# First chunks' queries in two loads, w_out's first piece ungated, and a moved conversion of w_in

## The chip, the cores and the metric

One core of a Trainium2 chip runs the kernel. The metric is the device time of one execution in microseconds (us), lower is better; the time of a kernel is the median of several runs. A core has five engines with an instruction queue each, which it works off in order: TensorE (PE, matmuls; PEld in the profile is its weight loads), VectorE (DVE), ScalarE (ACT), GpSimd (POOL) and SyncE (SP, which here issues nearly all transfers). They meet through semaphores. Tiles lie in SBUF (128 partitions), matmul results in PSUM banks.

## The reference: what is computed

The inputs are float32, except the two weight matrices: the reference multiplies them by a float64 scalar, so they arrive in 64 bits and the kernel converts them itself. An attention with sketched polynomial features is followed by an MLP with exact gelu:

```python
batch, n_heads, seq, head_dim = (4, 4, 1088, 32)     # r = 8 rows in S1 and S2
def phi(x):
    a = np.einsum('rd,bhsd->bhsr', S1, x)
    b = np.einsum('rd,bhsd->bhsr', S2, x)
    return np.einsum('bhsi,bhsj->bhsij', a, b).reshape(*x.shape[:-1], r * r)
q_p, k_p = (phi(q), phi(k))
kv = np.einsum('bhsf,bhsd->bhfd', k_p, v)
z = np.sum(k_p, axis=2)
num = np.einsum('bhsf,bhfd->bhsd', q_p, kv)
den = np.einsum('bhsf,bhf->bhs', q_p, z)[..., None] + 1e-06
x = (num / den).transpose(0, 2, 1, 3).reshape(B * S, H * D)      # 4352 x 128
h = x @ w_in                                                     # w_in 128 x 2048
g = 0.5 * h * (1.0 + erf(h / sqrt(2)))
out = g @ w_out                                                  # w_out 2048 x 128
```

The sum over the sequence needs every key and value of a batch element; each token of the queries is then independent.

## The kernel before

**Tiling.** The 1024 first tokens of each of the four batch elements are worked on in chunks of 512, two for each element (eight "main" chunks, numbered 0 to 7; 0 and 1 belong to element 0); the last 64 tokens of all elements make a ninth chunk. For each chunk the attention result `xT` (128 features x 512 tokens) is multiplied with w_in in 16 blocks of 128 hidden features (`hidden`, L715), ACT takes each block through gelu (L728), and the blocks are multiplied with w_out (`project`, L847, for the first blocks of chunks 0 and 1; products of a fast scheme, `two_products`, L794, for the others). `hidden` has two PSUM banks (`hidden_bank`, L77): the matmul of a block waits until the gelu of the block two before it has read its bank.

**Order.** The text of the kernel is the order on each engine: at the end (L1217 to L1224) each instruction is made to follow the one before it on its engine. The prologue (L887 to L961) is written out by hand, then a list of steps of one hidden block each is walked (L1164 to L1215), steps 0 to 3 being the first four blocks of chunk 0, with other work in between.

**Loads.** SP issues them in the order of L191 to L200: keys of element 0 (two transfers of two heads each), queries of chunk 0 (`load_q(0)`), values of element 0 (two), three small remainders, w_in's first piece, queries of chunk 1, w_in's second piece. `load_q` takes, for chunks 0 and 1, all four heads in one transfer with four tokens a partition, that is runs of 4 x 32 x 4 = 512 bytes; `load_main` (L99) does keys and values with eight tokens a partition, runs of 1 KB. Both weight matrices come in five pieces (L85: 256, 256, 512, 512 and 512 columns). `load_w_out(0, gated=True)` (L934) first has POOL write a word of the landing tile (L180), so that SP's transfer waits for POOL to get there; `load_rest` (L202) starts with w_out's second piece, gated too, and issues everything else behind it.

**Weights in 64 bits.** Class `Rounding` (L243) turns the raw words of a piece into float32 in steps that the caller places: `low_words` (ACT, L260), `fields` = `exponent_fields` and `mantissa_fields` (DVE, L268 and L273), `exponents` (ACT, L279, reads the exponent field), `mantissas` (DVE, L287, or by ACT and POOL, L284 and L285), `signs` (DVE, L292), `product` (DVE or another engine, L297). `finish` is the last three.

**The prologue.** Keys and queries of element 0 are turned on PE or DVE (`query_turn`, L520: a DVE transpose for chunk 0, four PE transposes for chunk 1), features are made, and kv of element 0 is summed. L939 to L960 then take chunk 0 through its numerators (`numerators_by_token`, L656), the denominators of its second half by ACT (L687), the division in two halves on DVE (`divide`, L673 to L679), and the turn of the result back to `xT` (first half: L702 and the copy L703 on ACT; second half: L694 and one copy each by ACT and DVE, L696). In between stand w_in's second piece (`w_in[1]`, its fields on both sides of the division's second half) and PE's expansion products for chunk 1 (L543). `first_hidden` (L730) is the first hidden block in halves. At steps 1 to 3 w_out's first two pieces are converted and chunk 1's numerators and division are done.

**Stores.** `store` (L860) writes chunks 0 and 1 in 16 transfers each of 16 KB, in runs of 32 floats; the row pattern follows from how tokens were spread over the partitions.

Of the kernel before, what the change touches and what calls it, by code (L numbers as in the profile page):

```python
# [8 lines left out]
FP = mybir.dt.float32  # L9
# [7 lines left out]
def kernel(  # L17
# [18 lines left out]
    pe, dve, act, pool, sp = nc.tensor, nc.vector, nc.scalar, nc.gpsimd, nc.sync  # L36
# [40 lines left out]
    def hidden_bank():  # L77
        return hps.tile([128, CW], FP, name="h_ps")
# [11 lines left out]
    rem = {n: big.tile([128, B // 2, H, D], FP, name=f"{n}_rem") for n in "kv"}  # L90
    q_rem = big.tile([128, 2, B // 2, 2, D], FP, name="q_rem")
    main = {(n, b): big.tile([128, H, J, D], FP, name=f"{n}_{b}") for n in "kv" for b in range(B)}
    q_sb = [big.tile([128, H, JC, D], FP, name=f"q_{n}") for n in range(NMAIN)]
    w_in_sb = [big.tile([d_model, c1 - c0], FP, name=f"w_in{i}") for i, (c0, c1) in enumerate(pieces)]
    w_out_sb = [big.tile([128, c1 - c0], FP, name=f"w_out{i}") for i, (c0, c1) in enumerate(pieces)]
    raw = {}
# [12 lines left out]
    def load_values(b):  # L109

        src = v[b, :, 0:MAIN, :].rearrange("h (t q n) d -> q t h (n d)", t=32, q=4)
        for g in range(4):
            sp.dma_start(out=main["v", b][g * 32:(g + 1) * 32].rearrange("t h n d -> t h (n d)"), in_=src[g])

    def load_q(n):
        at = n % NCH * CW
        if n < NCH:
            sp.dma_start(out=q_sb[n], in_=q[0, :, at:at + CW, :].rearrange("h (p j) d -> p h j d", j=JC))
            return
        for h in range(H):  # L120
            sp.dma_start(out=q_sb[n][h * 32:(h + 1) * 32].rearrange("t x j d -> t (x j d)"),
                         in_=q[n // NCH, h, at:at + CW, :].rearrange("(t n) d -> t (n d)", t=32))
# [47 lines left out]
    def load_w_in(i):  # L170
        src, e = words(moe_w_in)
        c0, c1 = pieces[i]
        sp.dma_start(out=landing(w_in_sb[i], e == 2), in_=src[:, c0 * e:c1 * e])
# [16 lines left out]
    nc.scalar.preload_act_table_set("gelu_and_others")  # L190
    for r in range(2):  # L191
        load_main(sp, "k", 0, slice(r, H, 2))
    load_q(0)
    for r in range(2):
        load_main(sp, "v", 0, slice(r, H, 2))
    for n, b in (("k", 0), ("k", 2), ("v", 0)):
        load_rem(n, b)
    load_w_in(0)
    load_q(1)
    load_w_in(1)  # L200

    def load_rest():  # L202

# [316 lines left out]
    def query_turn(n, copy=by_act):  # L520


        if n == 1:
            turned = transposed(work_bank(), "qT", [q_sb[1][:, h].rearrange("p j d -> p (j d)") for h in range(H)], copy)
            qT[n] = turned.rearrange("p (h j t) -> p h j t", h=H, j=JC)
            return
        qT[n] = att.tile([128, H, width[n] // 128, D], FP, name="qT" if n < NMAIN else "qT_rem")
        dve.transpose(out=qT[n].rearrange("p h j t -> p (h j t)"),
                      in_=q_sb[n].rearrange("p h j d -> p (h j d)") if n < NMAIN else q_rem.rearrange("p s b n d -> p (s b n d)"))

# [329 lines left out]
    def store(n):  # L860
# [10 lines left out]
        if n < NCH:  # L871

            for c in range(d_model // 32):
                to = out[row:row + CW, c * 32:(c + 1) * 32].rearrange("(g t j) d -> j t g d", t=32, j=JC)
                o = oT[c * 32:(c + 1) * 32].rearrange("p n (m d) -> p (n m) d", d=32)
                o = o.rearrange("p (g j) d -> j p g d" if n == 0 else "p (j g) d -> j p g d", j=JC)
                for j in range(JC):
                    sp.dma_start(out=to[j], in_=o[j])
            return
# [42 lines left out]
    kv_first_rem(kv_bank)  # L922
    w_in = [Rounding(w) for w in w_in_sb[:2]]
    w_in[0].low_words()
    w_in[0].fields()
    w_in[0].exponents()
    late = []
    query_turn(1, lambda **a: late.append(a))
# [2 lines left out]
    w_in[0].mantissas()  # L931
    w_in[0].signs()
    w_in[0].product(pool)
    load_w_out(0, gated=True)  # L934
    load_rest()
    w_out = [Rounding(w, beside=b) for w, b in zip(w_out_sb[:2], w_in)]
    by_act(**late[0])
    w_in[1].low_words()
    parts = [range(2), range(2, JC)]  # L939
    nd = [[hidden_bank(), hidden_bank()], [out_bank(), out_bank()]]  # L940
    for banks, tokens in zip(nd, parts):
# [1 line left out]
    den = denominators(nd[1])  # L943
    expand_products(1)
    divide(0, nd[0], parts[0], by_head_pair=True)
    w_in[1].exponent_fields()
    w_in[1].exponents()
    divide(0, nd[1], parts[1], by_head_pair=True, den=den)
    turn_half(0, 0, hidden_bank(), by_act)
    w_in[1].mantissa_fields()  # L950
    turn_half_apart(0, 1, [out_bank(), out_bank()])
    w_in[1].mantissas()
    w_in[1].signs()
    w_in[1].product()
    for half in range(2):
        first_hidden(0, half)
    for i in range(2):
        expand_copy(1, i)
    for i in range(2):
        expand_multiply(1, i)  # L960
    w_out[0].fields()  # L961


    steps = [(n, fi) for f in range(0, USUAL, 4) for n in range(NCH) for fi in range(f, f + 4)]
# [199 lines left out]
    for t in range(len(steps) + LAG):  # L1164
        if t < 4:

            hidden(0, t)
            if t == 1:
                w_out[0].low_words()
                w_out[0].exponents()  # L1170
                w_out[0].finish()
                w_out[1].fields()
            if t == 2:
                w_out[1].low_words()
            if t == 3:
                banks = work_banks()
                numerators_by_token(1, halves(banks), range(JC))
                w_out[1].mantissas(by_pool=True)
                w_out[1].exponents()
                divide(1, banks, range(JC), by_head_pair=False)  # L1180
                w_out[1].signs()
                w_out[1].product()
                project(0, 0)
                project(0, 1, cols=slice(0, 256))
                turn_half(1, 0, work_bank(), by_act)
                project(0, 1, cols=slice(256, 512))
                turn_half(1, 1, work_bank(), by_dve)
            continue
# [66 lines left out]
```

## Time and profile before

| What | us |
|---|---|
| time, median of 3 runs | 259.36 (259.24 to 259.5) |
| the profiled execution's span | 258.0 |
| PE busy in it | 253.9 (98%) |
| POOL, DVE, ACT busy | 163.5, 151.0, 115.5 |
| L721 matmuls (`hidden`), 514 of them | 136.9 |
| ACT's gelus L728 into `block`, 128 of them | 73.0 |
| POOL's sums L772 to L775, 28 each | 35.9, 35.7, 36.0, 35.8 |

All durations below are of the one profiled execution; the time of a run is the span and some 1.3 us around it. Times are counted from the span's start. In the timeline a row is a group of like instructions that follow each other: its start, its length, the engine, the line, what it writes and reads, how many; in brackets stands how long the engine was idle before it and whose work ended that. A float32 matmul shows as two instructions. Matmuls overlap, so that the start of the next one tells more than the length of one. A transfer's row on SP (SPq) is its issue; when it lands is told apart.

### The profile page before, as it was taken

Reading aid. Unit: us, or ns where it says so; the run is one execution under the profiler, and the core shown is the slowest. Engines: PE = TensorE matmul, PEld = TensorE weight load, DVE = VectorE, ACT = ScalarE, POOL = GpSimd, SP = SyncE. Lnnn points to the kernel's source line nnn. Section 1 sums busy time; section 2 is a strip of 40 time slices with the busy share of each in tenths; the row PEclk is TensorE's granted clock in tenths of the full one; section 3 lists DMA queues with packets and bytes.
Section 4 is the critical chain, followed back from the end, with each engine's and each line's share of the span. In section 5 each row is a group of like instructions: output and inputs, shape, how many; then the busy total and the mean of one; then the engine's idle time right before and its main releaser. Section 6 shows DMA issues by size and latency. Waiting matters only on the chain.

```text
span 258.0 us, 5769 instructions
## 1 busy us (share of the span) xinstructions
PE 253.9 (98%) x2335; PEld 136.1 (53%) x2335; DVE 151.0 (59%) x312; ACT 115.5 (45%) x224; POOL 163.5 (63%) x173
## 2 busy tenths in 40 slices
PE   8999999999999999999999999999999999999995
PEld 7856444345444545544444455455444444445794
DVE  2786888969699997590187986399307000700330
ACT  4685777443626332443335332533444334433442
POOL 3403006799968788487758775787758777877300
PEclk9999999999999999999999999999999999999999
DMA  6469848721000101102000002000200200020020
GB/s 199 144 185 374 188 95 217 213 76 14 3 0 12 31 1 21 23 6 37 3 0 3 0 9 38 0 1 3 41 3 4 39 0 1 7 36 0 3 41 20
DMA packets 29594, 13.48 MB, mean 52 GB/s; under 512 B 21888, under 2 KB 27776, under 8 KB 29568
## 3 DMA queue, kind: packets, MB, share of 16 engines
q1 hardware_dynamic: 29392, 13.05, 20.3%
q8 instruction: 18, 0.29, 0.5%
q10 hardware_dynamic: 176, 0.07, 0.1%
q14 instruction: 8, 0.07, 0.1%
HBM read 10.88 MB, written 2.23 MB: 51 GB/s over the span
## 4 chain that ended last, share of the span: by engine, by line
PE 98%; DVE 1%; issue 0%; ACT 0%; DVEq 0%
PE h_ps L721 45%; PE o_ps L807 33%; PE o_ps L858 5%; PE w_ps L855 3%; PE w_ps L437 1%; PE w_ps L890 1%; PE w_ps L578 1%; PE w_ps L633 1%; PE o_ps L426 1%; PE h_ps L737 1%; PE w_ps L978 1%; PE w_ps L656 0%; PE w_ps L543 0%; DVE x_tok L679 0%; PE h_ps L333 0%; PE w_ps L333 0%
## 5 line engine op out<-in xcount | busy, mean ns | idle before, releaser
L721 PE MATMUL h_ps<-xT,w_in 128*64 128x512 f32 (+3 forms) x514 | 136.9, 576 | 0.0
L728 ACT ACTIVATE block<-h_ps 128x512 f32<-128x512 f32 (+1 forms) x128 | 73.0, 571 | 117.3 <-PE h_ps L721 115.3
L721 PEld LDWEIGHTS h_ps<-xT,w_in 128*64 128x64 f32 (+1 forms) x514 | 41.9, 143 | 30.4 <-issue 11.6
L807 PE MATMUL o_ps<-block,w_out 128*64 128x256 f32 x224 | 57.5, 379 | 0.0
L772 POOL TENSOR_TENSOR bits_low<-block 128x512 f32<-128x512 f32 x28 | 35.9, 1281 | 27.8 <-ACT block L728 27.8
L807 PEld LDWEIGHTS o_ps<-block,w_out 128*64 128x64 f32 x224 | 30.5, 137 | 38.0 <-issue 27.5
L773 POOL TENSOR_TENSOR bits_a<-block 128x512 f32<-128x512 f32 x28 | 35.7, 1277 | 12.0 <-ACT block L728 11.9
L822 DVE COPY sums<-o_ps 64x256 f32<-64x256 f32 x8 | 3.3, 416 | 60.6 <-PE o_ps L807 60.6
L774 POOL TENSOR_TENSOR bits_e<-bits_a,block 128x512 f32<-128x512 f32 x28 | 36.0, 1286 | 2.2
L775 POOL TENSOR_TENSOR bits_m<-block,bits_e 128x512 f32<-128x512 f32 x28 | 35.8, 1279 | 2.2
L807 PE MATMUL o_ps<-bits_low,small 128*64 128x256 f32 x112 | 28.8, 380 | 0.0
L807 PE MATMUL o_ps<-bits_a,small 128*64 128x256 f32 x112 | 28.8, 380 | 0.0
L807 PE MATMUL o_ps<-block,small 128*64 128x256 f32 x112 | 28.8, 379 | 0.0
L807 PE MATMUL o_ps<-bits_m,w_out 128*64 128x256 f32 x112 | 28.8, 380 | 0.0
L807 PEld LDWEIGHTS o_ps<-block,small 128*64 128x64 f32 x112 | 15.2, 137 | 17.9 <-issue 10.8
L807 PE MATMUL o_ps<-bits_e,small 128*64 128x256 f32 x112 | 17.1, 383 | 0.0
L858 PE MATMUL o_ps<-g,w_out 128*128 128x512 f32 (+1 forms) x34 | 16.5, 572 | 0.0
L807 PEld LDWEIGHTS o_ps<-bits_m,w_out 128*64 128x64 f32 x112 | 15.4, 137 | 0.0
L807 PEld LDWEIGHTS o_ps<-bits_a,small 128*64 128x64 f32 x112 | 15.2, 137 | 0.0
L807 PEld LDWEIGHTS o_ps<-bits_low,small 128*64 128x64 f32 x112 | 15.2, 137 | 0.0
L590 DVE STREAM_TRANSPOSE w_ps<-w_ps 128x512 f32<-128x512 f32 (+1 forms) x7 | 4.8, 687 | 17.1 <-ACT xT L644 12.7
L807 PEld LDWEIGHTS o_ps<-bits_e,small 128*64 128x64 f32 x112 | 7.7, 137 | 10.6 <-issue 8.8
(194 smaller groups left out, 305.1 us busy)
## 6 DMA issues: line engine op xcount, KB each, us to landing
block<-in_moe_w_in_dram SPq DMA_DIRECT2D x3, 512.0 KB, 8.4
block<-in_moe_w_out_dram SPq DMA_DIRECT2D x3, 512.0 KB, 12.1
k<-in_k_dram SPq DMA_DIRECT2D x12, 128.0 KB, 3.1
v<-in_v_dram SPq DMA_DIRECT2D x12, 128.0 KB, 3.4
q<-in_q_dram SPq DMA_DIRECT2D x24, 64.0 KB, 2.4
out_dram<-oT SPq DMA_DIRECT2D x21, 64.0 KB, 2.2
k<-in_k_dram SPq DMA_DIRECT2D x2, 256.0 KB, 2.8
q<-in_q_dram SPq DMA_DIRECT2D x2, 256.0 KB, 3.9
```

The lines of the kernel that those rows point to most:

```text
L426: pe.matmul(ps[c * F:(c + 1) * F, r * 2 * D:r * 2 * D + C], lhsT=flat(k_p[0, r][:, t, c * 4 + ch * 2 + one]), rhs=v_aug[r][:, c, i, :C], s ...
L590: dve.transpose(out=tok, in_=ps[:, :, :H2])
L721: pe.matmul(ps[rows, :W], lhsT=w[:, rows], rhs=xT[n][:, :W], start=True, stop=True)
L728: act.activation(out=g_of[n, fi][:, :W], in_=ps[:, :W], func=ACT.Gelu)
L772: pool.tensor_sub(out=s[3], in0=a11, in1=a21)
L773: pool.tensor_add(out=s[1], in0=a21, in1=a22)
L774: pool.tensor_sub(out=s[2], in0=s[1], in1=a11)
L775: pool.tensor_sub(out=s[4], in0=a12, in1=s[2])
L807: pe.matmul(acc[n][bank][half * 64:(half + 1) * 64, col:col + HW], lhsT=fixed, rhs=moving, start=opens and e == 0 and name in "4715", stop ...
L822: dve.tensor_copy(out=N[lo, 0, one], in_=a0[lo, one])
L855: pe.matmul(o_of[n][i][:, :128], lhsT=g[:, i * 128:(i + 1) * 128], rhs=w_tile(w_out_sb, fi), start=first, stop=final)
L858: pe.matmul(o_of[n][:, cols], lhsT=w_tile(w_out_sb, fi), rhs=g[:, cols], start=first, stop=final)
```

## The change

Queries of chunks 0 and 1 get one tile, `q_first`, with eight tokens a partition, loaded in two transfers of two heads each (runs of 1 KB) where chunk 0's load stood; chunk n takes tokens 4n to 4n + 3 of each partition, chunk 0 is turned in two DVE transposes of two heads each, and the stores of both chunks follow the new token order. w_out's first piece is loaded without a gate, behind w_in's second piece. Of that piece (`w_in[1]`) the fields now follow those of `w_in[0]`, the exponents stand before the numerators of chunk 0, mantissas and signs behind the division, and the product is POOL's. w_out's first fields go before the two `expand_multiply`; at step 1 the conversion of w_out's first piece goes before `hidden(0, 1)`, and at step 3 that of its second piece up to the exponents before `hidden(0, 3)`. All matmuls stay as they are and in their order.

```diff
@@ -90,7 +90,9 @@
     rem = {n: big.tile([128, B // 2, H, D], FP, name=f"{n}_rem") for n in "kv"}
     q_rem = big.tile([128, 2, B // 2, 2, D], FP, name="q_rem")
     main = {(n, b): big.tile([128, H, J, D], FP, name=f"{n}_{b}") for n in "kv" for b in range(B)}
-    q_sb = [big.tile([128, H, JC, D], FP, name=f"q_{n}") for n in range(NMAIN)]
+    q_first = big.tile([128, H, J, D], FP, name="q_first")
+    q_sb = [q_first[:, :, n * JC:(n + 1) * JC] if n < NCH else big.tile([128, H, JC, D], FP, name=f"q_{n}")
+            for n in range(NMAIN)]
     w_in_sb = [big.tile([d_model, c1 - c0], FP, name=f"w_in{i}") for i, (c0, c1) in enumerate(pieces)]
     w_out_sb = [big.tile([128, c1 - c0], FP, name=f"w_out{i}") for i, (c0, c1) in enumerate(pieces)]
     raw = {}
@@ -112,11 +114,12 @@
         for g in range(4):
             sp.dma_start(out=main["v", b][g * 32:(g + 1) * 32].rearrange("t h n d -> t h (n d)"), in_=src[g])
 
+    def load_first_q(c):
+        heads = slice(2 * c, 2 * c + 2)
+        sp.dma_start(out=q_first[:, heads], in_=q[0, heads, 0:MAIN, :].rearrange("h (p j) d -> p h j d", j=J))
+
     def load_q(n):
         at = n % NCH * CW
-        if n < NCH:
-            sp.dma_start(out=q_sb[n], in_=q[0, :, at:at + CW, :].rearrange("h (p j) d -> p h j d", j=JC))
-            return
         for h in range(H):
             sp.dma_start(out=q_sb[n][h * 32:(h + 1) * 32].rearrange("t x j d -> t (x j d)"),
                          in_=q[n // NCH, h, at:at + CW, :].rearrange("(t n) d -> t (n d)", t=32))
@@ -190,14 +193,15 @@
     nc.scalar.preload_act_table_set("gelu_and_others")
     for r in range(2):
         load_main(sp, "k", 0, slice(r, H, 2))
-    load_q(0)
+    for c in range(NP):
+        load_first_q(c)
     for r in range(2):
         load_main(sp, "v", 0, slice(r, H, 2))
     for n, b in (("k", 0), ("k", 2), ("v", 0)):
         load_rem(n, b)
     load_w_in(0)
-    load_q(1)
     load_w_in(1)
+    load_w_out(0)
 
     def load_rest():
 
@@ -525,6 +529,12 @@
             qT[n] = turned.rearrange("p (h j t) -> p h j t", h=H, j=JC)
             return
         qT[n] = att.tile([128, H, width[n] // 128, D], FP, name="qT" if n < NMAIN else "qT_rem")
+        if n == 0:
+            for c in range(NP):
+                heads = slice(2 * c, 2 * c + 2)
+                dve.transpose(out=qT[n][:, heads].rearrange("p h j t -> p h (j t)"),
+                              in_=q_sb[n][:, heads].rearrange("p h j d -> p h (j d)"))
+            return
         dve.transpose(out=qT[n].rearrange("p h j t -> p (h j t)"),
                       in_=q_sb[n].rearrange("p h j d -> p (h j d)") if n < NMAIN else q_rem.rearrange("p s b n d -> p (s b n d)"))
 
@@ -871,7 +881,7 @@
         if n < NCH:
 
             for c in range(d_model // 32):
-                to = out[row:row + CW, c * 32:(c + 1) * 32].rearrange("(g t j) d -> j t g d", t=32, j=JC)
+                to = out[0:MAIN, c * 32:(c + 1) * 32].rearrange("(g t n j) d -> n j t g d", t=32, n=NCH, j=JC)[n]
                 o = oT[c * 32:(c + 1) * 32].rearrange("p n (m d) -> p (n m) d", d=32)
                 o = o.rearrange("p (g j) d -> j p g d" if n == 0 else "p (j g) d -> j p g d", j=JC)
                 for j in range(JC):
@@ -922,7 +932,8 @@
     kv_first_rem(kv_bank)
     w_in = [Rounding(w) for w in w_in_sb[:2]]
     w_in[0].low_words()
-    w_in[0].fields()
+    for w in w_in:
+        w.fields()
     w_in[0].exponents()
     late = []
     query_turn(1, lambda **a: late.append(a))
@@ -931,11 +942,11 @@
     w_in[0].mantissas()
     w_in[0].signs()
     w_in[0].product(pool)
-    load_w_out(0, gated=True)
     load_rest()
     w_out = [Rounding(w, beside=b) for w, b in zip(w_out_sb[:2], w_in)]
     by_act(**late[0])
     w_in[1].low_words()
+    w_in[1].exponents()
     parts = [range(2), range(2, JC)]
     nd = [[hidden_bank(), hidden_bank()], [out_bank(), out_bank()]]
     for banks, tokens in zip(nd, parts):
@@ -943,22 +954,19 @@
     den = denominators(nd[1])
     expand_products(1)
     divide(0, nd[0], parts[0], by_head_pair=True)
-    w_in[1].exponent_fields()
-    w_in[1].exponents()
     divide(0, nd[1], parts[1], by_head_pair=True, den=den)
+    w_in[1].mantissas()
     turn_half(0, 0, hidden_bank(), by_act)
-    w_in[1].mantissa_fields()
     turn_half_apart(0, 1, [out_bank(), out_bank()])
-    w_in[1].mantissas()
     w_in[1].signs()
-    w_in[1].product()
+    w_in[1].product(pool)
     for half in range(2):
         first_hidden(0, half)
     for i in range(2):
         expand_copy(1, i)
+    w_out[0].fields()
     for i in range(2):
         expand_multiply(1, i)
-    w_out[0].fields()
 
 
     steps = [(n, fi) for f in range(0, USUAL, 4) for n in range(NCH) for fi in range(f, f + 4)]
@@ -1164,19 +1172,19 @@
     for t in range(len(steps) + LAG):
         if t < 4:
 
-            hidden(0, t)
             if t == 1:
                 w_out[0].low_words()
                 w_out[0].exponents()
                 w_out[0].finish()
+            if t == 3:
+                w_out[1].low_words()
                 w_out[1].fields()
-            if t == 2:
-                w_out[1].low_words()
+                w_out[1].mantissas(by_pool=True)
+                w_out[1].exponents()
+            hidden(0, t)
             if t == 3:
                 banks = work_banks()
                 numerators_by_token(1, halves(banks), range(JC))
-                w_out[1].mantissas(by_pool=True)
-                w_out[1].exponents()
                 divide(1, banks, range(JC), by_head_pair=False)
                 w_out[1].signs()
                 w_out[1].product()
```

## The prediction

> **What bounds the kernel now.** I read the page's busy times, then the chain that ended last.
>
> ```profile
> PE 253.9 (98%) x2335; PEld 136.1 (53%) x2335; DVE 151.0 (59%) x312; ACT 115.5 (45%) x224; POOL 163.5 (63%) x173
> ...
> PE 98%; DVE 1%; issue 0%; ACT 0%; DVEq 0%
> ```
>
> TensorE (PE) is busy for 253.9 of 258.0 us and holds 98% of the chain. A change that leaves its matmuls as they are, as this one does, can win only time in which PE waits, and loses whatever new wait it makes. So I looked for PE's waits in the stretch that the diff touches. The chain in order of time (start, length, what) leaves PE once:
>
> ```profile
> 14.40 0.50 DVE x_tok L679 x2
> 14.90 0.14 issue
> 15.04 0.41 PE o_ps L694 x2
> 15.45 1.06 PE h_ps L737 x8
> 16.51 2.67 PE h_ps L721 x6
> 19.18 1.07 PE w_ps L656 x64
> ```
>
> Chunk 0's division on VectorE (DVE) holds PE up until 15.04. Before that, from 6.47 on, the single matmul rows follow each other without a wait; after 20.2 they do too, but for a tenth here and there. The timeline of all engines tells what each step hangs on (start, length, engine, line; in brackets idle time and who ended it):
>
> ```profile
> 13.90 0.28 DVE L268 TENSOR_SCALAR bits_e<-small 128x256 uint32<-128x256 uint32 x1
> ...
> 14.39 0.44 PE L702 MATMUL h_ps<-ident,x_tok 128*128 128x128 f32 x2
> ...
> 14.86 0.37 ACT L703 COPY xT<-h_ps 128x256 f32<-128x256 f32 x1
> ...
> 15.04 0.41 PE L694 MATMUL o_ps<-ident,x_tok 128*128 128x128 f32 x2 [0.21 <-DVE x_tok L679]
> ...
> 15.38 1.13 PE L737 MATMUL h_ps<-xT,w_in 128*128 128x128 f32 x8
> ...
> 16.55 0.60 ACT L728 ACTIVATE g<-h_ps 128x512 f32<-128x512 f32 x1
> ...
> 17.20 0.30 PEld L721 LDWEIGHTS h_ps<-xT,w_in 128*128 128x128 f32 x2 [0.65 <-ACT g L728]
> 17.41 0.60 ACT L728 ACTIVATE g<-h_ps 128x512 f32<-128x512 f32 x1 [0.26 <-PE h_ps L721]
> ...
> 17.90 0.42 ACT L260 ACTIVATE bits_low<-small 128x256 f32<-128x256 uint32 x1
> ...
> 18.06 0.30 PEld L721 LDWEIGHTS h_ps<-xT,w_in 128*128 128x128 f32 x2 [0.56 <-ACT g L728]
> ...
> 18.40 0.51 ACT L279 ACTIVATE bits_r<-bits_e,below 128x256 uint32<-128x256 uint32 x1
> ...
> 18.81 0.58 ACT L728 ACTIVATE g<-h_ps 128x512 f32<-128x512 f32 x1
> ```
>
> See the two weight loads of L721. `hidden` has two PSUM banks, so the matmul of feature block 2 waits for the gelu of block 0 (ends 17.15, load at 17.20), and that of block 3 for the gelu of block 1 (17.41 + 0.60 = 18.01, load at 18.06). Block 3 has nothing to spare: its weights go in just as block 2's matmuls finish.
>
> **Part 1: the loads.** The sync engine's (SP) issues at the start are these:
>
> ```profile
> 0.73 0.96 SPq L100 DMA_DIRECT2D k<-in_k_dram  x2
> 1.74 0.53 SPq L118 DMA_DIRECT2D q<-in_q_dram  x1
> 2.31 1.02 SPq L100 DMA_DIRECT2D v<-in_v_dram  x2
> ```
>
> By times to landing (2.7 and 2.9 for k, 4.2 for q, 4.3 and 4.6 for v) they land at 3.4, 4.1, 5.9, 6.6 and 7.4. A 256 KB load in runs of 1 KB thus takes 0.7 to 0.8 us behind the one ahead; q's 256 KB in runs of 512 bytes took 1.8. The new q loads are two of 256 KB in 1 KB runs. I estimate them at 0.75 each: landing at 4.9 and 5.6, v at 6.4 and 7.1, all 0.3 earlier than now. Nobody gains: DVE's q transpose starts at 5.92, right behind sT (5.74 + 0.16), and PE wants the result at 7.71, with 1 us to spare. Two transposes of half the size in place of one (0.71) may add a tenth on DVE, which afterwards idles 0.99. SP's issues up to w_in's first piece move back by one (0.5); remainders and w_in land by about 8 and 9 and are wanted at 9.35 and 10.6. w_in's second piece loses the q load ahead of it. w_out's first piece is issued near 7.1 and not 13.3, and lands near 10, wanted after 15. The later loads come 0.5 to 1 earlier. **Taken: 0.** Bounds: nothing to gain, since PE has no wait there; up to +0.5 if the loads come late (first rival).
>
> The Trainium skill, "DMA: Bandwidth & Descriptors" (Specifications), has runs of 512 bytes or more at line rate. By it the time would go by bytes and q's two loads would take 1.8 each; the rows above speak against it (0.7 to 0.8 for 1 KB runs, 1.8 for 512 bytes).
>
> **Part 2: chunk 0's division.** L268 for w_in's second piece (13.90 to 14.10 before the next starts) goes from between the reciprocals to before 12, where DVE has 0.54 idle ahead of 12.99. Then x_tok's second half is ready 0.19 sooner, 14.71 and not 14.90, and L694 starts near 14.85. ScalarE (ACT) now has L279 (0.41 to the next start) ahead of the denominators: 12.86 + 0.33 + 0.41 = 13.6 in place of 13.46, done at 13.85, just when DVE wants them (13.90). But L737, next on PE, waits for the copy of the *first* half: ACT L703 at 14.86 to 15.24, which follows PE's L702 (its result is out at 14.83), and L702 at 14.39 follows PE's own expansion matmuls. None of that moves. PE waits at L737 for what it no longer waits at L694. **Taken: 0**; bounds -0.19 (all passed on) and 0.
>
> **Part 3: w_in's second piece multiplied on GpSimd (POOL).** Mantissas now stand before DVE's copy L696 in time that was idle (0.39), signs after it: from 15.5 to 15.93. The product takes 0.73 on POOL (row of the first piece at 12.54) in place of 0.42, so 16.0 to 16.75. Its reader, block 2's matmul, cannot load weights before 17.20 (gelu of block 0). Cover 0.4. **Taken: 0**; bounds 0 and +1.1 (second rival).
>
> The Trainium skill, "SBUF — State Buffer" (Who interferes with whom), says that GpSimd and a VectorE instruction with two SBUF inputs, or in a two-port mode, lock each other out for a whole instruction. Rows agree in direction: beside L760 and L761 on POOL, DVE's L292 (43.99) took 0.94, against 0.69 at 26.79.
>
> **Part 4: ACT's order at the first gelus.** `w_out[0].low_words` and `exponents` now stand before `hidden(0, 1)`, and ACT is in order: gelu 0, L260, L279, gelu 1, gelu 2; before, the two came after gelu 1. By start-to-start rows: gelu 0.49 (17.41 to 17.90), L260 0.33 (19.29 to 19.62), L279 0.41 (18.40 to 18.81). Gelu 0 stays at 16.55 (PE's result at 16.51). L260 starts at 17.04, L279 at 17.37, and gelu 1 at 17.78 in place of 17.41: the idle 0.26 covers most of L260, L279 is behind it. Gelu 1 ends at 18.38, block 3's weights load at 18.43 in place of 18.06, and its matmuls come 0.37 late with PE idle. That L279 waits for DVE's L268 costs nothing more: the w_out fields are done by 16.3. Behind: chunk 1's numerators, division and first projection follow from those matmuls, so everything moves by the same 0.37, and DVE and ACT, which have w_out's pieces earlier than now, do not shorten it. **Taken: +0.37**; bounds 0 (PE catches up at a later wait) and +0.75 (nothing of L260 and L279 hidden).
>
> Then w_out's second piece goes before gelu 3 on ACT (three instructions, 1.2 us): gelu 3 near 20.0 in place of 19.6, wanted by the projection at 25.1. No cost. The stores' new strides keep 128-byte runs and lie at 81 to 106 us beside PE's work: 0. POOL's memset gone: 0.1 off the path.
>
> **Sum:** 0 + 0 + 0 + 0.37. The profiled execution's 258.0 becomes 258.4; around the span lie 1.3 us (259.36 median less 258.04), so **259.7 us**, +0.14%. A measurement of this kernel can tell about 0.2% (0.52 us) from no change, so the likeliest verdict is "within".
>
> **Rivals.**
> 1. *Query loads go by bytes.* Landing at 5.9 and 7.7, v at 8.4 and 9.2. The second transpose ends near 8.1 and PE's expansion, ready at 7.71, waits about 0.45; the remainders, 0.6 behind v, cost a tenth at 9.35. With part 4, +0.9: 260.2, slower than can be missed. It decides once the second q load lands after about 7.0. For it: q has the one slow row. Against: k and v, same shape and run as the new q. 0.08.
> 2. *The POOL product is late.* If DVE's fields and q_pT products (to 17.5) lock POOL out until 17.5, the product ends near 18.25 and block 2's weights load at 18.3, +1.1; block 3's 0.37 hides behind that: 260.5. It decides when the product ends after 17.15. Against: DVE and POOL lengthened each other by 0.2 to 0.4 in the rows, not by whole queues, and q_pT's products read PSUM. 0.06.
> 3. *PE catches up.* The waits of a tenth or so for weights at 43.1 to 52.8 (0.65 together) shrink because DVE and ACT, relieved early, are ahead of PE there; 0.37 comes back: 259.4, no slower. It needs those waits to hang on engines that PE does not pace; gelu rows there follow PE. 0.16.
> 4. *The division's 0.19 is passed on and ACT's order costs nothing* (gelu 0 early enough to take L279 as well: it would have to start by 16.2, its matmul ends at 16.51): 259.2. 0.05.
>
> That the loads and the order do not become what the diff says is excluded: the changed program's instruction order has two q loads of 128x2x256 and ACT's order as given.
>
> **Chances.** Forecast 0.60, rivals 0.08, 0.06, 0.16, 0.05, and 0.05 for what I do not see, half on each side. The forecast's own +0.37 has about 0.15 us of error from one profiled execution, which puts 0.12 of its 0.60 past +0.52. Slower by over 0.2%: 0.12 + 0.14 + 0.03 = 0.29; faster by over 0.2% (below 258.84): 0.05, as even rival 4 gains only 0.19; within: 0.66. The range, 259.1 to 260.3, takes in rivals 1, 3 and 4 and part 4's +0.75 and leaves rival 2 and the unseen.
>
> **What would show it.** In the changed kernel's profile: gelu 1 at 17.8 behind L260 and L279; a weight load of L721 at 18.4 with "ACT g" as releaser; L694 near 14.85 and L737 still near 15.38; POOL's product ending near 16.8; both q loads landed by 5.7. Wrong if PE's numerators of chunk 1 (L656, 19.11) do not start near 19.5, or if that delay is gone at 60 us.

## The result, and the profile after

The changed kernel took 260.0 us (median of 8 runs, 259.27 to 260.34) against 259.43 for the kernel before: ratio 1.0022, 95% interval [1.0012, 1.0031], that is +0.57 us [0.31, 0.80]. Run again later it gave 1.0033 [1.0019, 1.0048]. The unchanged kernel, measured against itself in the same way, gave 1.0008 [0.9999, 1.0018], which is not clear of 1. Taken as they are, the two results are a loss of 0.57 and 0.86 us; with 0.0008 taken off each they are 0.36 and 0.65. The forecast was +0.37.

The page of the changed kernel looks no worse than that of before:

```profile
span 257.8 us, 5767 instructions
PE 253.0 (98%) x2335; PEld 134.8 (52%) x2335; DVE 151.8 (59%) x312; ACT 115.0 (45%) x224; POOL 164.6 (64%) x173
```

The span is even 0.2 shorter than the 258.0 of before. This is the first thing to clear up, since the runs say that the kernel is slower. The timeline of PE at the turn of the keys shows it, first before, then after (start, length, engine, line, what, how many):

```profile
3.79 1.06 PE L333 MATMUL h_ps<-ident,k 128*128 128x128 f32 x4
```

```profile
3.78 0.60 PE L337 MATMUL h_ps<-ident,k 128*128 128x128 f32 x4
```

The same four matmuls start at the same time and take 1.06 in the one execution and 0.60 in the other. The trace's first record of the full granted clock (1.0) starts at 6.91 in the profile of before and at 3.77 in that of after, and until then PE runs at about half its pace. (The page's PEclk row shows 9 in all slices of both.) The unchanged kernel's second profile has it at 5.64, so no fixed start belongs to either kernel. Chunk 0's numerators therefore start at 11.28 and not 12.28, and whole spans cannot be compared. What can be compared are stretches behind that point. I use three marks, all starts of PE matmuls: chunk 0's first numerator (L656, after L666), the first hidden matmul (L737, L747), the first projection (L858, L868). **Stretch A** is from the first to the second mark (the division lies in it), **stretch B** from the second to the third (the first gelus). From the projection to the end of the span all fourteen profiled executions of this study took 237.85 to 237.90, so everything is decided before 21 us. Between the two profiles A went from 3.11 to 3.43, B from 4.80 to 5.20; with the start 1.00 earlier: 258.04 - 1.00 + 0.32 + 0.40 = 257.76, the span within 0.05.

Stretch B first. The timeline of after:

```profile
15.91 0.63 ACT L738 ACTIVATE g<-h_ps 128x512 f32<-128x512 f32 x1
...
16.39 0.46 ACT L264 ACTIVATE bits_low<-small 128x256 f32<-128x256 uint32 x1
...
16.65 0.30 PEld L731 LDWEIGHTS h_ps<-xT,w_in 128*128 128x128 f32 x2 [0.78 <-POOL w_in L301]
...
16.72 0.53 ACT L283 ACTIVATE bits_r<-bits_e,below 128x256 uint32<-128x256 uint32 x1
...
17.12 1.29 ACT L738 ACTIVATE g<-h_ps 128x512 f32<-128x512 f32 x2
...
17.78 0.30 PEld L731 LDWEIGHTS h_ps<-xT,w_in 128*128 128x128 f32 x2 [0.84 <-ACT g L738]
```

ACT's order is gelu 0, L264, L283, gelu 1, and block 3's weights wait for gelu 1. The two loads of L731 stand 1.13 apart, against 0.86 before (17.20 and 18.06). The first of them is a little late as well: it comes 0.11 behind the end of gelu 0 (16.54), against 0.05 before.

Stretch A. The chain that ended last, in order of time, now leaves PE for a transfer:

```profile
6.60 4.91 DMA small<-in_moe_w_in_dram
...
13.82 0.50 DVE x_tok L689 x2
14.32 0.14 issue
14.45 0.41 PE o_ps L704 x2
14.86 0.98 PE h_ps L747 x8
15.84 1.94 PE h_ps L731 x4
```

DVE's timeline tells why:

```profile
11.53 0.30 DVE L272 TENSOR_SCALAR bits_e<-small 128x256 uint32<-128x256 uint32 x1 [0.94 <-DMA small<-in_moe_w_in_dram]
11.74 0.29 DVE L277 TENSOR_SCALAR bits_a<-small 128x256 uint32<-128x256 uint32 x1
11.94 0.42 DVE L291 SCALAR_TENSOR_TENSOR bits_m<-bits_a,bits_low 128x256 f32<-128x256 uint32 x1
12.28 0.42 DVE L296 SCALAR_TENSOR_TENSOR bits_e<-small,bits_r 128x256 uint32<-128x256 uint32 x1
12.62 0.22 DVE L683 TENSOR_SCALAR den_tok<-h_ps 128x4 f32<-128x4 f32 x2
```

The moved fields of w_in's second piece (L272 and L277, from 11.53 on) wait for that piece, which landed at 11.51 (10.37 in the profile of before); the first piece's L291 and L296 and then the denominators stand behind them in DVE's queue. The denominators start 1.34 behind chunk 0's first numerator, which is the row at 11.28:

```profile
11.28 0.67 PE L666 MATMUL h_ps<-kz,q_pT 64*64 64x33 f32 x32
```

In the profile of before it was 0.71, and DVE waited for PE there:

```profile
12.28 0.67 PE L656 MATMUL h_ps<-kz,q_pT 64*64 64x33 f32 x32
12.99 0.23 DVE L673 TENSOR_SCALAR den_tok<-h_ps 128x4 f32<-128x4 f32 x2 [0.54 <-PE h_ps L656]
```

### The profile page after: what moved, and what is told of

It reads as the page before. It is cut to its first block, busy times and chain, and to the rows that moved or that the text cites. A ratio compares the mean times of both kernels' runs of the same rounds, so it can differ in the third digit from the quotient of the medians.

```text
span 257.8 us, 5767 instructions
## 1 busy us (share of the span) xinstructions
PE 253.0 (98%) x2335; PEld 134.8 (52%) x2335; DVE 151.8 (59%) x312; ACT 115.0 (45%) x224; POOL 164.6 (64%) x173
## 4 chain that ended last, share of the span: by engine, by line
PE 93%; SPq 2%; DMA 2%; DVE 1%; issue 0%; ACT 0%; DVEq 0%
PE h_ps L731 45%; PE o_ps L817 33%; PE o_ps L868 5%; PE w_ps L865 3%; DMA small<-in_moe_w_in_dram 2%; PE w_ps L441 1%; PE w_ps L588 1%; PE w_ps L643 1%; SPq L135 1%; PE h_ps L747 1%; SPq L102 1%; PE w_ps L986 1%; PE w_ps L666 0%; DVE x_tok L689 0%; SPq L119 0%
## 5 line engine op out<-in xcount | busy, mean ns | idle before, releaser
L731 PE MATMUL h_ps<-xT,w_in 128*64 128x512 f32 (+3 forms) x514 | 137.2, 576 | 0.0
L731 PEld LDWEIGHTS h_ps<-xT,w_in 128*64 128x64 f32 (+1 forms) x514 | 41.8, 142 | 30.9 <-issue 11.3
L817 PEld LDWEIGHTS o_ps<-block,small 128*64 128x64 f32 x112 | 15.1, 137 | 18.0 <-issue 10.6
L868 PE MATMUL o_ps<-g,w_out 128*128 128x512 f32 (+1 forms) x34 | 16.5, 572 | 0.0
L817 PEld LDWEIGHTS o_ps<-bits_e,small 128*64 128x64 f32 x112 | 7.7, 137 | 10.6 <-issue 8.8
```

The costliest lines, as they stand in the source:

```text
L731: pe.matmul(ps[rows, :W], lhsT=w[:, rows], rhs=xT[n][:, :W], start=True, stop=True)
L817: pe.matmul(acc[n][bank][half * 64:(half + 1) * 64, col:col + HW], lhsT=fixed, rhs=moving, start=opens and e == 0 and name in "4715", stop ...
L868: pe.matmul(o_of[n][:, cols], lhsT=w_tile(w_out_sb, fi), rhs=g[:, cols], start=first, stop=final)
```

## The experiments

My theory after the result: stretch B is longer because of ACT's order, in every execution (part 4); stretch A is longer when w_in's second piece lands late, which happens by chance when w_out's first piece is not held back (parts 1 and 2 together). Rivals: the query loads hold PE up; the product on POOL does; the pace of PE does. The table has the marks of one profiled execution of each kernel and the ratio of its runs to runs of the kernel before that were taken beside them; "held" says whether w_out's first piece is held back, "landed" when w_in's second piece did.

| Kernel | full pace from | numerators | held, landed | A | B | ratio |
|---|---|---|---|---|---|---|
| before | 6.91 | 12.28 | yes, 10.37 | 3.11 | 4.80 | |
| after | 3.77 | 11.28 | no, 11.51 | 3.43 | 5.20 | 1.0022 [1.0012, 1.0031] |
| e1 | 5.39 | 11.69 | no, 10.24 | 3.11 | 4.86 | 1.0008 [0.9999, 1.0018] |
| e2 | 3.63 | 11.78 | yes, 10.14 | 3.11 | 5.14 | 1.0010 [1.0001, 1.0019] |
| e3 | 4.50 | 11.37 | no, 10.17 | 3.58 | 5.15 | 1.0019 [1.0007, 1.0030] |
| e4 | 6.59 | 12.13 | yes, 10.77 | 3.11 | 5.15 | 1.0016 [1.0007, 1.0026] |
| e5 | 6.72 | 12.34 | yes, 10.42 | 3.11 | 4.80 | 1.0008 [0.9995, 1.0020] |
| e6 | 6.00 | 11.90 | no, 10.43 | 3.11 | 5.14 | 1.0032 [1.0021, 1.0044] |
| e7 | 6.97 | 12.30 | no, 12.88 | 3.78 | 4.86 | 1.0023 [1.0010, 1.0036] |
| e8 | 5.64 | 11.72 | yes, 10.81 | 3.11 | 4.80 | 1.0008 [0.9999, 1.0018] |
| e9 | 5.15 | 12.02 | no, 10.96 | 3.22 | 5.15 | 1.0033 [1.0019, 1.0048] |
| e10 | 5.26 | 11.59 | no, 11.28 | 3.11 | 5.14 | (profile alone) |
| e11 | 5.88 | 11.91 | yes, 10.18 | 3.11 | 4.80 | 1.0002 [0.9988, 1.0017] |
| e12 | 5.72 | 11.76 | no, 10.87 | 3.11 | 4.80 | 1.0001 [0.9989, 1.0013] |

**ACT's order alone (e4), and undone (e1).** e4 is the kernel before with part 4 at step 1 and the earlier w_out fields:

```diff
+    w_out[0].fields()
     for i in range(2):
         expand_multiply(1, i)
-    w_out[0].fields()
...
-            hidden(0, t)
             if t == 1:
                 w_out[0].low_words()
                 w_out[0].exponents()
                 w_out[0].finish()
+            hidden(0, t)
+            if t == 1:
                 w_out[1].fields()
```

> The kernel before with one part of the change: w_out's first fields ahead of the two expand_multiply, and at step 1 the conversion of its first piece ahead of hidden(0, 1). Theory A: gelu 1 starts behind the two conversion instructions, second stretch 5.15 to 5.25 in place of 4.80, first stretch 3.11 within 0.05, time +0.37 us (+0.14%) on the kernel before. Rivals B and C: second stretch 4.8 to 4.9, time within 0.1 us of before. A held-back w_out piece lands near 16.4 us here, which may add a little to the second stretch.

B went from 4.80 to 5.15. The timeline of e4 shows the order at work:

```profile
16.41 0.60 ACT L728 ACTIVATE g<-h_ps 128x512 f32<-128x512 f32 x1
16.90 0.43 ACT L260 ACTIVATE bits_low<-small 128x256 f32<-128x256 uint32 x1
17.23 0.49 ACT L279 ACTIVATE bits_r<-bits_e,below 128x256 uint32<-128x256 uint32 x1
17.63 1.18 ACT L728 ACTIVATE g<-h_ps 128x512 f32<-128x512 f32 x2
```

And e4's weight loads of `hidden`:

```profile
17.05 0.30 PEld L721 LDWEIGHTS h_ps<-xT,w_in 128*128 128x128 f32 x2 [0.65 <-ACT g L728]
18.27 0.30 PEld L721 LDWEIGHTS h_ps<-xT,w_in 128*128 128x128 f32 x2 [0.92 <-ACT g L728]
```

Gelu 1 starts 1.22 after gelu 0, against 0.86 in the profile of before (16.55, 17.41): +0.36. Block 3's weights wait for it: the second load comes 1.22 behind the first, which had followed gelu 0. The time of e4 (1.0016) alone is not clear of that of the unchanged kernel (1.0008); it is the stretch that shows the effect.

e1 is the changed kernel with the two exchanged again at step 1:

```diff
-            if t == 1:
-                w_out[0].low_words()
-                w_out[0].exponents()
-                w_out[0].finish()
             if t == 3:
...
             hidden(0, t)
+            if t == 1:
+                w_out[0].low_words()
+                w_out[0].exponents()
+                w_out[0].finish()
```

> The changed kernel with one thing undone: at step 1 the conversion of w_out's first piece stands behind hidden(0, 1) again. I read two stretches of PE's matmul starts: the first from chunk 0's numerators (into h_ps) to first_hidden, before 3.11 us, changed 3.43; the second from there to the first projection, before 4.80, changed 5.20. Theory A (ScalarE's order at the first gelus costs the second stretch its 0.40): second stretch back to 4.80 within 0.05, first stretch stays wherever the loads put it (3.1 to 3.45), time 0.4 us under the changed kernel. Rival B (the cost is w_in's second piece landing late and holding up VectorE): second stretch may shorten, but the time stays within 0.15 us of the changed kernel's. Rival C (the GpSimd product holds block 2 up): second stretch stays above 4.95.

B fell to 4.86. Its timeline has gelu 1 ahead of L264, with the idle time of before in front:

```profile
15.96 0.60 ACT L738 ACTIVATE g<-h_ps 128x512 f32<-128x512 f32 x1
16.82 0.60 ACT L738 ACTIVATE g<-h_ps 128x512 f32<-128x512 f32 x1 [0.26 <-PE h_ps L731]
17.32 0.43 ACT L264 ACTIVATE bits_low<-small 128x256 f32<-128x256 uint32 x1
17.64 0.50 ACT L283 ACTIVATE bits_r<-bits_e,below 128x256 uint32<-128x256 uint32 x1
```

All kernels with the new order have B at 5.14 to 5.20, all others at 4.80 to 4.86, in fourteen executions without an exception. In the times, the six kernels with it (after, e2, e3, e4, e6, e9) have a mean ratio of 1.0022, the six without (e1, e5, e7, e8, e11, e12) 1.0008: a difference of 0.0014 x 259.4 = 0.36 us. (The two groups differ in other parts of the change too, so this agrees with the stretch but does not show it by itself.)

**The queries alone (e5), and undone (e6).** e5 is the kernel before with `q_first`, its two loads, the two half transposes and the new store rows:

```diff
-    load_q(0)
+    for c in range(NP):
+        load_first_q(c)
...
     load_w_in(0)
-    load_q(1)
     load_w_in(1)
```

> The kernel before with the query part of the change alone: two loads of eight tokens a partition, two half transposes, the new rows in the stores. Theory A: nothing PE waits for moves; both query loads land by 6.3 us, w_in's second piece by 10 us, both stretches as before (3.11 and 4.80 within 0.05), time within 0.15 us of before. Rival D (the query loads delay what follows): values or remainders late, PE's expansion or key matmuls wait, chunk 0's numerators start over 0.3 us later at the same pace of the first matmuls, time +0.3 us or more.

The second load landed at 7.26, and DVE had to wait for it:

```profile
7.28 0.45 DVE L534 STREAM_TRANSPOSE qT<-q_first 128x256 f32<-128x256 f32 x1 [0.84 <-DMA q_first<-in_q_dram]
```

PE's expansion, which reads both transposes, took 1.21 from its start to the next step, against 1.05 in each of the six executions with the loads of before. In e2 (full pace from 3.63, second load at 6.44) and e9 (5.15 and 6.95) it took 1.72 and 1.51, in the other six with the new loads 1.05 to 1.21. So the loads can cost up to 0.67 where PE is early and they are late, and then they take back what PE had won by its early pace. Over the eight profiles with the new loads that is 0.2 on average; the time of e5, though, is that of the unchanged kernel. e6 is the changed kernel with these edits taken back:

```diff
-    for c in range(NP):
-        load_first_q(c)
+    load_q(0)
...
     load_w_in(0)
+    load_q(1)
     load_w_in(1)
```

> The changed kernel with the query part undone: chunk 0's and chunk 1's queries loaded apart in runs of 512 bytes, at their old places. If the new query loads cost time (in the run of the query part alone the second one landed at 7.26 us and PE's expansion of chunk 0 waited 0.16; in the gated run at 6.44 with PE earlier, and it waited 0.64), then PE's expansion matmuls of chunk 0 take 1.05 us again, values land by 7.0, and the time is 0.1 to 0.3 us under the changed kernel. If they cost nothing, as forecast, the time is the changed kernel's within 0.1. The second stretch stays at 5.1 to 5.2 by either.

1.0032: nothing of the loss goes when the queries are loaded as before, so no cost of the query loads shows in the times.

**w_out's first piece held back again (e2), and let go alone (e12).**

```diff
     load_w_in(1)
-    load_w_out(0)
...
+    load_w_out(0, gated=True)
     load_rest()
```

> The changed kernel with one thing undone: w_out's first piece is held back by GpSimd again, ahead of the second. Theory A: the second stretch stays at 5.2, the first is back to 3.1 because w_in's second piece lands before 10.4 us and no longer holds VectorE up; time between that of the changed kernel and 0.3 us under it, depending on how early PE reaches chunk 0's division. Rival B (the late landing is the main cause): time 0.4 us or more under the changed kernel. If w_in's second piece still lands after 11 us, the ungated w_out load is not what delays it.

A is 3.11 and w_in's second piece lands at 10.14; B stays at 5.14. The ratio, 1.0010, is below those of the other kernels with ACT's new order that let the piece go (1.0019 to 1.0033), but the intervals overlap or touch, except that of e6. e12 lets it go in the kernel before (the same edit the other way):

> The kernel before with one part of the change alone: w_out's first piece is issued behind w_in's second piece and not held back. Theory: a piece of 256 KB at that point costs by chance, in two ways: w_in's second piece lands later than 10.9 in about half of the executions (here harmless, since VectorE wants it only at 13.4 or later), and PE's matmuls stop inside chunk 0's numerators, after the 23rd, for 0.1 to 0.5 us in some three of seven. The gelu stretch stays 4.80, the division's stretch is 3.11 or 3.2 to 3.6; ratio 1.0005 to 1.0020. Rival: w_out's earlier transfer costs nothing, as the prediction had it: 3.11, ratio 1.0002 to 1.0008, as the unchanged kernel gave.

1.0001: here no cost of the early transfer is seen, below what the theory expected and a little below the rival's 1.0002 to 1.0008 (the interval goes up to 1.0013). That w_in's second piece landed at 10.87 was harmless, since DVE wants it only at 13.39. For a late landing to cost time, it takes the moved fields as well.

**The product on DVE (e3).**

```diff
-    w_in[1].product(pool)
+    w_in[1].product()
```

> The changed kernel with one thing undone: the product of w_in's second piece is VectorE's again. In the trace of the run with step 1 put back, block 2's weights of L731 load 0.11 us after gelu 0 ends, against 0.05 in the kernel before: the wait for ScalarE stands in a semaphore instruction of its own and the weight load waits for GpSimd. Theory A (as amended): block 2 comes 0.86 us after block 1 in place of 0.94 to 1.00; block 3 is still held up by gelu 1, so the second stretch shrinks by 0.1 at most, to 5.1 to 5.2; time within 0.15 us of the changed kernel. Rival C (the product on GpSimd is itself late): second stretch 5.0 or less.

Blocks 1 and 2 are again 0.86 apart (0.94 in e1, e2, e6, e9 and e10 with POOL's product), but block 3 waits for gelu 1 as before and B is 5.15: POOL's product costs 0.06 where ACT's order is the old one (e1: 4.86 against 4.80) and nothing on top of the new one. (e7, without that product, shows 4.86 too: there gelu 0 ended 0.86 behind the start of its matmul, against 0.80 in before and e1, and why is open.) A was 3.58, for a reason that I had not thought of. PE's timeline:

```profile
11.37 0.55 PE L666 MATMUL h_ps<-kz,q_pT 64*64 64x33 f32 x23
12.19 0.32 PE L666 MATMUL h_ps<-kz,q_pT 64*64 64x33 f32 x9 [0.28 <-issue]
```

PE stops after the 23rd numerator with no semaphore to wait for ("issue"). The same place shows a gap of 496 ns between starts here, 516 in e7, 134 in e9, and at most 40 in the other eleven executions. The 0.47 by which A is longer here is this stop.

**ACT's order, the product and the queries taken back (e7).** The diffs of e1, e3 and e6 together, so that the early transfer, the moved fields, the moved exponents and mantissas and the order at step 3 are left.

> The changed kernel with step 1's order, the product and the query loads put back; w_out's first piece still not held back, w_in's second fields still outside the division. Theory A and the amended costs of the queries and the product together: second stretch 4.80, first 3.11, time that of the kernel before within 0.15 us. If the ungated load or the moved fields cost something of their own, it is slower than before by 0.2 us or more; if they are worth something, faster by 0.2.

1.0023, and A of 3.78: a loss stays without ACT's order, without the query loads and without POOL's product. It is not the same in every execution: the profiled one took 260.58, one of three above 260.3, while the other nine took 259.24 to 259.92. DVE's timeline:

```profile
11.33 0.28 DVE L274 TENSOR_SCALAR bits_a<-small 128x256 uint32<-128x256 uint32 x1
12.90 0.29 DVE L269 TENSOR_SCALAR bits_e<-small 128x256 uint32<-128x256 uint32 x1 [1.29 <-DMA small<-in_moe_w_in_dram]
13.11 0.29 DVE L274 TENSOR_SCALAR bits_a<-small 128x256 uint32<-128x256 uint32 x1
13.31 0.42 DVE L288 SCALAR_TENSOR_TENSOR bits_m<-bits_a,bits_low 128x256 f32<-128x256 uint32 x1
13.65 0.42 DVE L293 SCALAR_TENSOR_TENSOR bits_e<-small,bits_r 128x256 uint32<-128x256 uint32 x1
13.99 0.22 DVE L674 TENSOR_SCALAR den_tok<-h_ps 128x4 f32<-128x4 f32 x2
```

DVE takes up the denominators 1.69 after the numerators' start (12.30), against 0.72 in e11 and 0.71 in before. PE's stop, 0.5 of it, lies beneath the longer wait for the transfer.

**Controls: the kernel before (e8), the changed one (e9, e10), and the changed one without its three costs (e11).**

> The kernel before, unchanged. Five profiles show PE's first key transposes at 0.21 us each, as at half pace, and full pace from between 3.6 and 6.9 us on, whichever kernel it is. If that is chance of the execution, this one has a full-pace start somewhere in that stretch too, its time from the first key transposes to chunk 0's numerators follows it, and the ratio is 1 within 0.1%. If full pace from 6.9 belongs to the kernel before, it is 6.6 to 6.9 again.

> The changed kernel as it is, profiled once more. Theory: what the change costs in every execution is ACT's order alone, first projection to block 1 at 5.15 to 5.20 us against 4.80; the late landing of w_in's second piece is a matter of chance, so the stretch from chunk 0's numerators to its first hidden matmul is 3.11 when that piece lands before 10.9 and about 3.4 when it lands near 11.5. The start of PE's full pace falls anywhere from 3.6 to 7.0. Ratio 1.0015 to 1.0030. Rival A: the late landing is built into the changed kernel: the stretch is 3.4 again, the landing 11.4 or later. Rival B: the change sets the start of the full pace: 3.7 to 3.9 again.

> The same program a third time, for the same three numbers. Theory: 5.15 to 5.20 for the gelu stretch; 3.11 or 3.4 for the division's stretch as the landing of w_in's second piece has it (before 10.9 or after); full pace anywhere from 3.6 to 7.0. Rival A: 3.4 and a landing of 11.4 or later. Rival B: full pace at 3.7 to 3.9.

> The changed kernel with ACT's order of before, w_out's first piece held back again and w_in's second product on DVE: of the change are left the query loads, the earlier fields and mantissas. Theory: w_in's second piece lands at 10.1 to 10.8, the division's stretch is 3.11, the gelu stretch 4.80 with blocks at 0.86 and 0.95 from each other, so no difference from before but the wait for the second query load: ratio 1.0000 to 1.0010. Rival: the earlier field of w_in's second piece brings the 0.19 of the division through after all: stretch 2.92, ratio under 0.9998.

e8 gave 1.0008, the same A and B, and another start of the full pace. e9 and e10 settle the two rivals of the repeated runs: neither A (3.43, 3.22, 3.11 for the same program) nor the pace (3.77, 5.15, 5.26) is built into the changed kernel; B is (5.20, 5.15, 5.14). In e10 the piece landed at 11.28 and A was still 3.11, since the numerators were late too (11.59): DVE came to the denominators 0.79 behind them. In after it was 1.34, in e7 1.69, and A is longer by 0.32 and 0.67: what goes beyond 1.02 is paid, in both. e9's 0.11 is PE's stop. e11 is e1, e2 and e3 in one: A 3.11, B 4.80, 1.0002, no difference from before. Its PE timeline shows what the moved fields bring:

```profile
14.47 0.41 PE L703 MATMUL o_ps<-ident,x_tok 128*128 128x128 f32 x2
15.02 1.13 PE L746 MATMUL h_ps<-xT,w_in 128*128 128x128 f32 x8
```

From the numerators at 11.91, the turn of the second half comes after 2.56 (2.76 in before: 12.28 to 15.04), the hidden matmul after the same 3.11. No kernel here is faster than before.

**What the packet records add.** Both ways in which A grew go back to one thing that the theory did not name, the loading of the program's own instructions. The pages have a queue for it, next to the queue of SP's transfers:

```profile
q8 instruction: 18, 0.29, 0.5%
```

These are 18 packets of 16 KB. In each of the fourteen executions the first of them that falls into this prologue starts between 8.82 and 10.81 and takes 0.96 us (1.39 in e5).

- *The late landing.* In after, e10 and e7 this packet ends at 10.01, 9.78 and 11.77. In each of the three, a packet of w_in starts within 0.02 of that end, some of those behind it take 0.23 in place of 0.08, and from 11.0 on (10.9 in e7, 10.6 in e10) at most two packets at a time are in flight, against 14 to 17 at 9.6. So what came last of the piece was a share that stood behind the instruction packet: its last packet ended 1.08, 1.08 and 0.64 behind that end. In the other eleven executions w_in's last packet ended before the instruction packet did, and the piece landed by 10.96.
- *PE's stop.* In e3, e9 and e7 the packet ends at 10.90, 11.20 and 11.77, and the 24th numerator starts 1.29, 1.28 and 1.37 behind that end. In the other eleven executions it starts 1.29 to 2.21 behind it, and there is no stop. So PE stopped just where its 24th numerator would otherwise have come sooner than some 1.3 behind the packet's end.

The records show this order in time in all fourteen executions; no experiment moved the instruction packet by itself.

## Why the prediction was right, and where it was not

The forecast, +0.37 from ACT's order and nothing from the rest, was right in its sign and in its main term, and the measured 260.0 lies 0.3 above its 259.7. The second term that the runs point to was costed at nothing. The +0.57 is a little more than the 0.52 that the prediction took for the least that a measurement can tell.

- **Part 4: right, in mechanism and size.** Gelu 1 behind L264 and L283, block 3's weights behind it: +0.35 in e4, +0.34 to +0.40 in all, 0.37 on record. The delay is not given back (rival 3, PE catches up): from the projection on, all kernels take the same 237.9. Block 3 waited in every kernel with the new order, so rival 4 falls as well. Chunk 1's numerators, which the prediction wanted near 19.5, start at 18.84 in after; put back by the start that came 1.00 earlier and freed of A's 0.32 that is 19.52.
- **Part 1: loads mis-sized, path right.** The first query load landed 1.2 to 1.8 behind the last of the keys, not 0.75, and the second at 6.2 to 7.3, not 5.6. Rival 1's condition (after 7.0) was met in one execution, e5, where PE waited 0.16 and not 0.45; in after the wait was 0.02, and e5's time is that of the control. But the condition was put wrongly: with PE early it waited 0.67 at a landing of 6.44 (e2), beyond the bound of +0.5, and 0.46 at 6.95 (e9), so what counts is when PE comes. The Trainium skill, "DMA: Bandwidth & Descriptors" (Specifications), by which runs of 512 bytes and more go at line rate, is not refuted by the row that I held against it: q's first load was slow in runs of 1 KB too, 1.22 to 1.80 behind the keys in eight executions, against 1.69 to 2.04 in five of the six with runs of 512 bytes (in e12, where the keys landed late, 0.74). How much of the difference is the length of the runs is not shown.
- **Parts 1 and 2 together: the step that failed.** The prediction put the moved field "before 12, where DVE has 0.54 idle" and took 0 for it, without a landing time for w_in's second piece (the 9 that it names for w_in, wanted at 10.6, is the first piece's, which landed at 9.74 in after); of w_out's first piece it asked only whether its own reader has it in time. The second piece landed at 11.51, since a share of it stood behind an instruction packet, and in order behind the field stood the whole division: A +0.32 in after. The price is a matter of chance. Of the eight executions with the early transfer w_in's second piece landed after 10.9 in four (and at 10.87 in e12), of the six without in none; A was over 3.11 in four of the seven that had the moved field as well (after and e7 by the landing, e3 and e9 by PE's stop; the mean of the seven is 3.33), in none of the other seven. Where the times are sorted so (after the fact, and with intervals that overlap), the four results with these two and ACT's order (after, e3, e6, e9) have a mean ratio of 1.0027, e2 and e4 1.0013; without ACT's order, the two with them (e1, e7) have 1.0016, the four others (e5, e8, e11, e12) 1.0005.
- **Part 2's own step: right.** The turn of the second half (L704, there L703) comes 0.20 sooner in e11 (0.19 on record), and the hidden matmul (L747, there L746) does not move: it starts at 15.02, behind the first half's copy on ACT (14.50 to 14.87).
- **Part 3: right but for 0.06.** POOL's product ended at 16.33 in after, before gelu 0 (16.54), but the weight load then came at 16.65 and not 0.05 behind that gelu. The lock that the prediction spoke of is there: beside POOL's product (15.61, 0.72) DVE's L277 took 0.85 in after, 0.84 in e9, and 0.29 in e11, where the product is DVE's. The Trainium skill, "SBUF — State Buffer" (Who interferes with whom), has the one that comes second wait for the whole instruction, where a VectorE instruction in a two-port mode meets GpSimd; L277 started 0.03 behind POOL's and ended 0.16 after it, which agrees in the main (whether L277 runs in such a mode, no view says). It is off the path.

**What stays open:** what the early transfer has to do with it. The instruction packet started between 8.82 and 10.81 in the eight executions with the early transfer and between 9.42 and 9.81 in the six without; a late landing behind it was seen in three of the eight and PE's stop in three, both in none of the six. That goes together, but it is one execution each, and no kernel moved the packet or the transfer's place in the queue by itself. The cause of stretch B is shown by e4 and e1; the cause of stretch A is read from the traces.

## What to carry to other kernels

On an engine that works in order, a conversion put ahead of an evacuation delays what the evacuation frees: count the engine's instructions between two releases of the same pair of banks, and leave out only as much as its idle time there covers. A step that is moved up to fill idle time takes its own transfer's landing with it as a new condition, and everything behind it in the queue inherits that; so the scatter of the landing counts, not one profile's value. Where a landing is late or an engine stops without a semaphore, look for an instruction packet in the DMA records of that moment. Where two profiles differ in the start, compare stretches between marks, not spans.

## What the runs showed of the hardware

- **The start of PE's full pace is a matter of chance.** In fourteen executions, with the same warm-up matmuls from 0.77 on, it came anywhere from 3.63 to 6.97 us, and chunk 0's numerators from 11.28 to 12.34, mostly with it (in e2 and e9 PE waited for the queries); that is more than the whole effect studied. The Trainium skill, "TensorE: Matmul & The Clock Gate" (Part 1), has a free-running window of 3.4 us that must be busy; a scatter of 3.34 fits a window of that length with a random phase, though the earliest start, 2.86 behind the first matmul, leaves no whole window behind that matmul. The 0.5 us either way that the same part gives for the scatter does not fit.
- **The first load of the queries is slow, whatever its runs.** The first 256 KB of q in 1 KB runs landed 1.2 to 1.8 behind the last of k, the second 0.7 to 1.5 behind the first; the first 256 KB of v, in the same runs, landed 0.7 to 1.2 behind the query load ahead of them. In the packet records single packets of the first loads took 0.3 to 1.2 us, the median packet of 1 KB 0.046. Why is open.
- **An instruction packet of 16 KB takes 0.96 us, and a transfer's share can stand behind it**: in after, e7 and e10 w_in's second piece landed 1.1 to 1.5 behind such a packet's end.
- **PE can stop with no wait**: gaps of 134 to 516 ns at the same instruction in e3, e7 and e9, which ended 1.28 to 1.37 behind the end of such a packet.
